# Cosformer attention feeding a leaky-relu feed-forward: 96 partitions of 6 tokens, one-pass leaky relu, and a hand-written order of all engines, on one Trainium2 core

## The chip, the cores and the metric

The kernel runs on one core of a Trainium2 chip. The metric is the device time of one execution in microseconds, measured outside the profiler; the profile's span of the same execution is about 2 us shorter. Ratios are the mean time of one kernel's fast runs over the mean time of the other's fast runs of the same rounds, so they are not quite the ratio of the medians that are quoted.

Names: PE is TensorE's matmul side and PEld its weight loads, DVE is VectorE, ACT is ScalarE, POOL is GpSimd, SP is SyncE. `L204` is line 204 of the kernel in question. Line numbers differ between kernels. In the attention, `kp` and `qp` are phi(k) and phi(q), made by the k and q prep passes; `vex` is v in 16 bit, made by `vcast`; `den`, `rden` and `xs` are the denominator, its reciprocal and the quotient.

## The reference, cut to what matters

```python
# q, k, v: (8 batches, 8 heads, 576 tokens, 64); w_in: (512, 2048); w_out: (2048, 512), all float32
theta = np.pi / 2 * np.arange(S) / S
def phi(x):                                   # 64 -> 128 features
    r = np.maximum(x, 0.0)
    return np.concatenate([r * cos(theta), r * sin(theta)], axis=-1)
kv  = einsum('bhsf,bhsd->bhfd', phi(k), v)    # per head 128 x 64
z   = phi(k).sum(axis=2)
num = einsum('bhsf,bhfd->bhsd', phi(q), kv)
den = einsum('bhsf,bhf->bhs', phi(q), z)[..., None] + 1e-6
x   = (num / den).transpose(0, 2, 1, 3).reshape(4608, 512)
h   = x @ w_in
out = np.maximum(0.01 * h, h) @ w_out
```

The feed-forward is the large part: 9 groups of 512 tokens, each with 64 matmuls for the first layer and 64 for the second. A batch of 576 tokens is a little longer than a group, so attention of batch g+1 must be finished before the first layer of group g+1 begins.

## The kernel before

Attention splits 576 tokens into two chunks of 128 partitions x 2 tokens and one of 64 x 1. For each piece `q` is transposed on PE (`ps_qt`), copied to SBUF (`qpT`), multiplied with `kv` (`pnum`), divided on VectorE (`xs`), transposed back (`ps_xt`) and copied into `xT`. The feed-forward needs two passes for the leaky relu, has three PSUM banks for the first layer (`psh`) and one for the second (`pso`). A scheduler orders the instructions of all engines.

```python
psh_pool = ctx.enter_context(tc.tile_pool(name="ps_h", bufs=3, space=PSUM))
pso_pool = ctx.enter_context(tc.tile_pool(name="ps_o", bufs=1, space=PSUM))
# ... cut ...
def emit_b1(t):                               # first layer of group t
    for m in range(NFT):                      # 16 tiles of 4 matmuls
        psh = psh_pool.tile([P, GRP], dt.float32, name="psh")
        # ... 4 matmuls into psh ...
        hsb = hpool.tile([P, GRP], dt.float32, name="hsb")
        nc.scalar.copy(hsb, psh)
        g = gpool.tile([P, GRP], dt.float16, name="g")
        nc.vector.scalar_tensor_tensor(
            out=g, in0=psh, scalar=0.01, in1=hsb, op0=ALU.mult, op1=ALU.max)
def emit_b2(t, gs):                           # second layer
    for tt in range(4):
        pso = pso_pool.tile([P, DM], dt.float32, name="pso")
        # ... 16 matmuls into pso ...
        osb = opool.tile([P, DM], dt.float32, name="osb")
        nc.vector.tensor_copy(osb, pso)       # then stored to DRAM
# ... cut ...
for bb in range(B + 1):                       # the main loop
    # ... issue loads: k, v of batch bb+1, q of batch bb; with bb == 0 all weights as well ...
    if bb >= 1: phase2(bb - 1, q_stage[bb - 1])      # q side of attention
    if bb < B:  phase1(bb, *kv_stage[bb])            # k, v side
    while groups_done < NGRP and (groups_done + 1) * GRP <= bb * S:
        gs_ = emit_b1(groups_done); emit_b2(groups_done, gs_); groups_done += 1
```

Of the kernel before, what the change touches and what calls it, by code (L numbers as in the profile page):

```python
# [9 lines left out]
dt = mybir.dt  # L11
# [3 lines left out]
P = 128  # L15
# [3 lines left out]
def kernel(  # L19
# [15 lines left out]
    assert F == P and DM == 4 * P and DFF % P == 0 and NT % 512 == 0  # L35
    assert S == 576

    chunk3 = [(0, P, 2), (2 * P, P, 2), (4 * P, S - 4 * P, 1)]
    JMAX = 2
    subs = []  # L40
    for c_, (s0_, npc_, Jc_) in enumerate(chunk3):
        for j_ in range(Jc_):
            subs.append((c_, j_, npc_))
    NSUB = len(subs)
    NC3 = len(chunk3)

    def slot_base(c, j):
        s0, npc, Jc = chunk3[c]
        return s0 + j * npc
# [5 lines left out]
    NE = D + 2  # L55

    const = ctx.enter_context(tc.tile_pool(name="const", bufs=1))
    ident32 = const.tile([P, P], dt.float32, name="ident32")
    make_identity(nc, ident32)
    ident16 = const.tile([P, P], dt.float16, name="ident16")  # L60
    nc.vector.tensor_copy(ident16, ident32)

    w_ang = math.pi / 2.0 / S
    bias_pi2 = const.tile([P, 1], dt.float32, name="bias_pi2")
# [3 lines left out]
    iotaA = const.tile([P, 2, 2], dt.float32, name="iotaA")  # L68
    nc.gpsimd.iota(
        iotaA,  # L70
        pattern=[[2 * P, 2], [1, 2]],
        base=0,
        channel_multiplier=2,
        allow_small_or_imprecise_dtypes=True,
    )
    iotaB = const.tile([P, 1], dt.float32, name="iotaB")
    nc.gpsimd.iota(
        iotaB,
        pattern=[[1, 1]],
        base=4 * P,  # L80
        channel_multiplier=1,
        allow_small_or_imprecise_dtypes=True,
    )
    cosA = const.tile([P, 2, 2], dt.float32, name="cosA")
    sinA = const.tile([P, 2, 2], dt.float32, name="sinA")
    nc.scalar.activation(cosA, iotaA, AF.Sin, bias=bias_pi2, scale=w_ang)
    nc.scalar.activation(sinA, iotaA, AF.Sin, bias=bias_zero, scale=w_ang)
    ntail = chunk3[2][1]
    cosB = const.tile([P, 1], dt.float32, name="cosB")
    sinB = const.tile([P, 1], dt.float32, name="sinB")  # L90
    nc.scalar.activation(
        cosB[0:ntail], iotaB[0:ntail], AF.Sin, bias=bias_pi2[0:ntail], scale=w_ang
    )
    nc.scalar.activation(
        sinB[0:ntail], iotaB[0:ntail], AF.Sin, bias=bias_zero[0:ntail], scale=w_ang
    )

    def cos_col(c, j, npc):
        return cosA[0:npc, c, j : j + 1] if c < 2 else cosB[0:npc, 0:1]

    def sin_col(c, j, npc):
        return sinA[0:npc, c, j : j + 1] if c < 2 else sinB[0:npc, 0:1]

    xT = const.tile([P, NKC, NT], dt.float16, name="xT")
    onesJ = const.tile([P, H, JMAX, 2], dt.float32, name="onesJ")
    nc.vector.memset(onesJ, 1.0)

    w1 = const.tile([P, NKC, DFF], dt.float16, name="w1")
    w2 = const.tile([P, NFT, DM], dt.float16, name="w2")

    def load_w1_slice(c):
        nc.gpsimd.dma_start(w1[:, c, :], moe_w_in[c * P : (c + 1) * P, :])

    def load_w2_slices(ms):
        for m in ms:
            nc.gpsimd.dma_start(w2[:, m, :], moe_w_out[m * P : (m + 1) * P, :])

    kstage = ctx.enter_context(tc.tile_pool(name="kstage", bufs=NC3 + 1))
    vstage = ctx.enter_context(tc.tile_pool(name="vstage", bufs=NC3 + 1))
    qstage = ctx.enter_context(tc.tile_pool(name="qstage", bufs=NC3 + 2))  # L120
    vexpool = ctx.enter_context(tc.tile_pool(name="vext", bufs=1))
    kppool = ctx.enter_context(tc.tile_pool(name="kpp", bufs=NC3 + 2))
    qppool = ctx.enter_context(tc.tile_pool(name="qpp", bufs=NC3))
    qptpool = ctx.enter_context(tc.tile_pool(name="qpT", bufs=4))
    kvpool = ctx.enter_context(tc.tile_pool(name="kvsb", bufs=2))
    xpool = ctx.enter_context(tc.tile_pool(name="xs", bufs=4))
    small = ctx.enter_context(tc.tile_pool(name="small", bufs=3))
    hpool = ctx.enter_context(tc.tile_pool(name="hsb", bufs=2))
    gpool = ctx.enter_context(tc.tile_pool(name="gpool", bufs=NFT + 3))
    opool = ctx.enter_context(tc.tile_pool(name="osb", bufs=2))  # L130
    pskx = ctx.enter_context(tc.tile_pool(name="ps_kvx", bufs=1, space=bass.MemoryType.PSUM))
    psqt = ctx.enter_context(tc.tile_pool(name="ps_qt", bufs=1, space=bass.MemoryType.PSUM))
    psnum = ctx.enter_context(tc.tile_pool(name="ps_num", bufs=1, space=bass.MemoryType.PSUM))
    psh_pool = ctx.enter_context(tc.tile_pool(name="ps_h", bufs=3, space=bass.MemoryType.PSUM))
    pso_pool = ctx.enter_context(tc.tile_pool(name="ps_o", bufs=1, space=bass.MemoryType.PSUM))

    vex_sets = []
    for parity in range(2):
        sset = []
        for c, (s0, npc, Jc) in enumerate(chunk3):  # L140
            vx = vexpool.tile(
                [P, H, Jc, NE], dt.float16, name=f"vex_{parity}_{c}", uniquify=False
            )
            nc.vector.tensor_copy(vx[0:npc, :, :, D:NE], onesJ[0:npc, :, 0:Jc, :])
            sset.append(vx)
        vex_sets.append(sset)

    kv_tiles = {}
    kv_stage = {}
    q_stage = {}  # L150

    def issue_kv_loads(b):
        ksts = []
        vsts = []
        for c, (s0, npc, Jc) in enumerate(chunk3):
            kst = kstage.tile([P, H, Jc, D], dt.float32, name="kst")
            nc.sync.dma_start(  # L157
                kst[0:npc],
                k[b, :, s0 : s0 + Jc * npc, :].rearrange(
                    "h (p j) d -> p h j d", j=Jc  # L160
                ),
            )
            vst = vstage.tile([P, H, Jc, D], dt.float32, name="vst")
            nc.sync.dma_start(  # L164
                vst[0:npc],
                v[b, :, s0 : s0 + Jc * npc, :].rearrange(
                    "h (p j) d -> p h j d", j=Jc
                ),
            )
            ksts.append(kst)  # L170
            vsts.append(vst)
        return ksts, vsts

    def issue_q_loads(b):
        qsts = []
        for c, (s0, npc, Jc) in enumerate(chunk3):
            qst = qstage.tile([P, H, Jc, D], dt.float32, name="qst")
            nc.sync.dma_start(
                qst[0:npc],
                q[b, :, s0 : s0 + Jc * npc, :].rearrange(  # L180
                    "h (p j) d -> p h j d", j=Jc
                ),
            )
            qsts.append(qst)
        return qsts

    def phase1(b, ksts, vsts):
        kps = []
        vexs = []
        for c, (s0, npc, Jc) in enumerate(chunk3):  # L190
            kp = kppool.tile([P, H, Jc, F], dt.float16, name="kp")
            for j in range(Jc):
                nc.scalar.activation(  # L193
                    kp[0:npc, :, j, 0:D],
                    ksts[c][0:npc, :, j, :],
                    AF.Relu,
                    bias=bias_zero[0:npc],
                    scale=cos_col(c, j, npc),
                )
                nc.vector.tensor_scalar(  # L200
                    out=kp[0:npc, :, j, D:F],
                    in0=ksts[c][0:npc, :, j, :],
                    scalar1=0.0,
                    scalar2=sin_col(c, j, npc),  # L204
                    op0=ALU.max,
                    op1=ALU.mult,
                )
            kps.append(kp)
            vex = vex_sets[b % 2][c]
            nc.vector.tensor_copy(vex[0:npc, :, :, 0:D], vsts[c][0:npc])  # L210
            vexs.append(vex)
        kv_sb = kvpool.tile([P, H, NE], dt.float16, name="kv_sb")
        for hg in range(2):
            ps_kv = pskx.tile([P, 4, NE], dt.float32, name="ps_kv", tag="pskx")
            for hh in range(4):
                h = hg * 4 + hh
                for i, (c, j, npc) in enumerate(subs):
                    nc.tensor.matmul(  # L218
                        ps_kv[:, hh, :],
                        lhsT=kps[c][0:npc, h, j, :],  # L220
                        rhs=vexs[c][0:npc, h, j, :],
                        start=(i == 0),
                        stop=(i == NSUB - 1),
                    )
            nc.scalar.copy(kv_sb[:, hg * 4 : hg * 4 + 4, :], ps_kv)
        kv_tiles[b] = kv_sb
# [208 lines left out]
```

## Time and profile before

| | |
|---|---|
| median time, first measurement (3 runs) | 388.69 us |
| first attention matmul / first feed-forward matmul | 30.73 us / 55.79 us |
| 64 second-layer matmuls of a group at full pace | 4 x 3.45 us = 13.8 us |
| last matmul to end of span | 4.5 us |
| mean granted TensorE clock | 0.989 |

The first lines are from the profile page: busy time of the engines, then the chain of work that ended last (followed back from the last instruction to what released each step), by engine and by line.

```profile
...
PE 329.0 (85%) x2272; PEld 172.6 (44%) x2272; DVE 218.2 (56%) x454; ACT 173.8 (45%) x285; POOL 11.7 (3%) x28
...
PE 79%; DVE 6%; SPq 6%; DMA 4%; ACT 3%; issue 1%; ACTq 0%
PE psh L343 34%; PE pso L363 33%; PE ps_kv L218 5%; DVE osb L371 4%; SPq L164 3%; PE ps_qt L257 3%; DMA kst<-in_k_dram 3%; PE ps_xt L296 3%; SPq L157 2%; ACT qpT L263 2%; PE pnum L270 2%; DMA qst<-in_q_dram 1%; DVE xs L284 1%; ACT xT L302 1
...
```

PE holds 79% of the chain. Its two feed-forward lines are 67% of the span; no other engine comes near. The VectorE copy `osb` (L371) stands in the chain with 4%, which means that PE work was released by it. Next, groups of instructions from the same page: engine, operation, shapes, count, then busy time and mean ns of one, then idle time of the engine before them.

```profile
...
L353 DVE SCALAR_TENSOR_TENSOR g<-psh,hsb 128x512 f16<-128x512 f32 x144 | 97.9, 688 | 33.2 <-ACT hsb L351 32.1
L351 ACT COPY hsb<-psh 128x512 f32<-128x512 f32 x144 | 83.2, 585 | 50.8 <-PE psh L343 48.9
...
L371 DVE COPY osb<-pso 128x512 f32<-128x512 f32 x36 | 24.9, 692 | 87.7 <-PE pso L363 87.7
L263 ACT COPY qpT<-ps_qt 128x1024 f16<-128x1024 f16 (+1 forms) x40 | 37.1, 929 | 54.9 <-PE ps_qt L257 53.8
...
```

The leaky relu costs 585 ns on ACT and then 688 ns on DVE per tile; a tile's four matmuls take 0.864 us on PE. Last, what PE itself waited for (total us, times, longest), and a stretch of the timeline (start, duration, engine and line, count, wait before).

```profile
...
PE ps_kv L218 <- DVE kp L200: 31.3, 4, 30.7
PE ps_qt L257 <- ACT qpT L263: 10.3, 11, 1.2
PE pso L363 <- DVE osb L371: 4.7, 9, 0.8
...
```

```profile
...
122.84 0.42 PE L270 MATMUL pnum<-kv_sb,qpT 128*128 128x66 f16 x8
123.19 0.41 PE L257 MATMUL ps_qt<-ident_63,qp 64*128 64x64 f16 x8
123.78 3.61 PE L363 MATMUL pso<-w_85,g 128*128 128x512 f16 x16 [0.19 <-DVE osb L371]
127.23 0.39 PE L296 MATMUL ps_xt<-ident_63,xs 128*128 128x128 f16 x4
127.45 0.42 PE L270 MATMUL pnum<-kv_sb,qpT 128*128 128x66 f16 x8
...
```

When the 16 matmuls of one `pso` tile are done, PE does a few attention matmuls (`pnum`, `ps_qt`, `ps_xt`) while VectorE copies the tile, and so it hardly waits: 4.7 us in nine waits. The VectorE copy `osb` is on the chain with about 16.7 us.

### The profile page before, as it was taken

Reading aid. Unit: us, or ns where it says so; the run is one execution under the profiler, and the core shown is the slowest. Engines: PE = TensorE matmul, PEld = TensorE weight load, DVE = VectorE, ACT = ScalarE, POOL = GpSimd, SP = SyncE. Lnnn points to the kernel's source line nnn. Section 1 sums busy time; section 2 is a strip of 40 time slices with the busy share of each in tenths; the row PEclk is TensorE's granted clock in tenths of the full one; section 3 lists DMA queues with packets and bytes.
Section 4 is the critical chain, followed back from the end, with each engine's and each line's share of the span. In section 5 each row is a group of like instructions: output and inputs, shape, how many; then the busy total and the mean of one; then the engine's idle time right before and its main releaser. Section 6 shows DMA issues by size and latency. Waiting matters only on the chain.

```text
span 388.8 us, 5799 instructions
## 1 busy us (share of the span) xinstructions
PE 329.0 (85%) x2272; PEld 172.6 (44%) x2272; DVE 218.2 (56%) x454; ACT 173.8 (45%) x285; POOL 11.7 (3%) x28
## 2 busy tenths in 40 slices
PE   0004479997899999989999999899999999999984
PEld 0003455455444554455455545554455455444431
DVE  0006858945696369555955783566467427733711
ACT  3014556624583248326832672455256426612600
POOL 6230000000000000000000000000000000000000
PEclk9999999999899999998999999999999999999999
DMA  8999998567572418232604302100120031011022
GB/s 203 214 212 306 338 311 193 158 187 207 149 206 64 110 29 235 74 112 69 189 29 110 81 0 56 67 2 1 56 54 2 3 73 36 0 54 56 1 55 54
DMA packets 71003, 42.31 MB, mean 109 GB/s; under 512 B 14656, under 2 KB 65856, under 8 KB 70976
## 3 DMA queue, kind: packets, MB, share of 16 engines
q1 hardware_dynamic: 68096, 37.76, 35.4%
q0 software_dynamic: 2880, 4.20, 5.9%
q8 instruction: 17, 0.28, 0.3%
q14 instruction: 10, 0.08, 0.1%
HBM read 36.70 MB, written 9.44 MB: 119 GB/s over the span
## 4 chain that ended last, share of the span: by engine, by line
PE 79%; DVE 6%; SPq 6%; DMA 4%; ACT 3%; issue 1%; ACTq 0%
PE psh L343 34%; PE pso L363 33%; PE ps_kv L218 5%; DVE osb L371 4%; SPq L164 3%; PE ps_qt L257 3%; DMA kst<-in_k_dram 3%; PE ps_xt L296 3%; SPq L157 2%; ACT qpT L263 2%; PE pnum L270 2%; DMA qst<-in_q_dram 1%; DVE xs L284 1%; ACT xT L302 1%; ACT kp L193 0%
## 5 line engine op out<-in xcount | busy, mean ns | idle before, releaser
L343 PE MATMUL psh<-xT,w_84 128*128 128x512 f16 x576 | 139.0, 387 | 0.2
L363 PE MATMUL pso<-w_85,g 128*128 128x512 f16 x576 | 133.2, 379 | 5.9 <-DVE osb L371 4.7
L353 DVE SCALAR_TENSOR_TENSOR g<-psh,hsb 128x512 f16<-128x512 f32 x144 | 97.9, 688 | 33.2 <-ACT hsb L351 32.1
L351 ACT COPY hsb<-psh 128x512 f32<-128x512 f32 x144 | 83.2, 585 | 50.8 <-PE psh L343 48.9
L363 PEld LDWEIGHTS <-g 128*128 128x128 f16 x576 | 56.2, 98 | 71.7 <-issue 8.4
L343 PEld LDWEIGHTS <-w_84 128*128 128x128 f16 x576 | 54.0, 99 | 61.7 <-issue 3.6
L371 DVE COPY osb<-pso 128x512 f32<-128x512 f32 x36 | 24.9, 692 | 87.7 <-PE pso L363 87.7
L263 ACT COPY qpT<-ps_qt 128x1024 f16<-128x1024 f16 (+1 forms) x40 | 37.1, 929 | 54.9 <-PE ps_qt L257 53.8
L218 PE MATMUL ps_kv<-vex_0,kp 128*128 128x66 f16 x128 | 15.5, 204 | 31.8 <-DVE kp L200 30.9
L302 ACT COPY xT<-ps_xt 128x512 f16<-128x512 f16 (+1 forms) x40 | 21.8, 545 | 44.4 <-PE ps_xt L296 43.7
L257 PE MATMUL ps_qt<-ident_63,qp 128*128 128x128 f16 (+1 forms) x320 | 26.3, 225 | 14.6 <-ACT qpT L263 10.3
L218 PEld LDWEIGHTS <-kp 128*128 128x128 f16 (+1 forms) x320 | 19.3, 99 | 42.7 <-issue 33.8
L193 ACT ACTIVATE kp<-kst,bias_zero,cosA 128x512 f16<-128x512 f32 x32 | 25.7, 818 | 19.2 <-DMA kst<-in_k_dram 19.2
L257 PEld LDWEIGHTS <-qp 128*128 128x128 f16 (+1 forms) x320 | 20.8, 103 | 19.2 <-issue 11.7
L284 DVE TENSOR_TENSOR xs<-pnum,rden 128x512 f16<-128x512 f32 (+1 forms) x40 | 27.4, 686 | 0.8
L270 PE MATMUL pnum<-kv_sb,qpT 128*128 128x66 f16 (+1 forms) x320 | 19.1, 202 | 0.0
L296 PE MATMUL ps_xt<-ident_63,xs 128*128 128x128 f16 (+1 forms) x160 | 16.1, 228 | 2.0 <-DVE xs L284 2.0
L296 PEld LDWEIGHTS <-xs 128*128 128x128 f16 (+1 forms) x160 | 11.1, 103 | 13.2 <-DVE xs L284 6.5
L270 PEld LDWEIGHTS <-qpT 128*128 128x128 f16 (+1 forms) x320 | 15.7, 107 | 2.7 <-issue 0.4
L235 DVE TENSOR_SCALAR qp<-qst,cosA 128x512 f16<-128x512 f32 x32 | 15.2, 474 | 1.6 <-PE ps_qt L257 0.8
L218 PE MATMUL ps_kv<-vex_1,kp 128*128 128x66 f16 x128 | 15.0, 199 | 0.4 <-DVE kp L200 0.4
L200 DVE TENSOR_SCALAR kp<-kst,sinA 128x512 f16<-128x512 f32 x32 | 14.3, 476 | 1.6 <-DMA kst<-in_k_dram 1.6
(34 smaller groups left out, 96.1 us busy)
## 6 DMA issues: line engine op xcount, KB each, us to landing
kst<-in_k_dram SPq DMA_DIRECT2D x16, 512.0 KB, 5.0
vst<-in_v_dram SPq DMA_DIRECT2D x16, 512.0 KB, 6.0
qst<-in_q_dram SPq DMA_DIRECT2D x16, 512.0 KB, 4.6
out_dram<-osb SPq DMA_DIRECT2D x40, 128.0 KB, 2.4
out_dram<-osb SPq DMA_DIRECT2D x16, 256.0 KB, 2.5
w_84<-in_moe_w_in_dram POOLq DMA_DIRECT2D x4, 512.0 KB, 10.3
w_85<-in_moe_w_out_dram POOLq DMA_DIRECT2D x16, 128.0 KB, 7.3
kst<-in_k_dram SPq DMA_DIRECT2D x8, 128.0 KB, 4.6
```

Of the source, the lines that this page charges most:

```text
L193: nc.scalar.activation(kp[0:npc, :, j, 0:D], ksts[c][0:npc, :, j, :], AF.Relu, bias=bias_zero[0:npc], scale=cos_col(c, j, npc),)
L218: nc.tensor.matmul(ps_kv[:, hh, :], lhsT=kps[c][0:npc, h, j, :], rhs=vexs[c][0:npc, h, j, :], start=(i == 0), stop=(i == NSUB - 1),)
L257: nc.tensor.transpose(ps_qt[:, h, 0:npc], qp[0:npc, h, j, :], ident16[0:npc, 0:npc],)
L263: nc.scalar.copy(qpT[:, :, 0:npc], ps_qt[:, :, 0:npc])
L270: nc.tensor.matmul(pnum[0:npc, h // 4, (h % 4) * NE : (h % 4) * NE + NE], lhsT=qpT[:, h, 0:npc], rhs=kv_sb[:, h, :],)
L284: nc.vector.tensor_tensor(out=xs[0:npc].rearrange("p (a b) e -> p a b e", a=2), in0=pnum[0:npc, :, 0 : 4 * NE].rearrange("p a (b e) -> p a ...
L296: nc.tensor.transpose(ps_xt[:, jj, 0:npc], xs[0:npc, 2 * jj : 2 * jj + 2, :], ident16[0:npc, 0:npc],)
L343: nc.tensor.matmul(psh, lhsT=w1[:, c, m * P : (m + 1) * P], rhs=xT[:, c, t * GRP : (t + 1) * GRP], start=(c == 0), stop=(c == NKC - 1),)
L351: nc.scalar.copy(hsb, psh)
L353: nc.vector.scalar_tensor_tensor(out=g, in0=psh, scalar=0.01, in1=hsb, op0=ALU.mult, op1=ALU.max)
L363: nc.tensor.matmul(pso, lhsT=gs[m][:, tt * P : (tt + 1) * P], rhs=w2[:, m, :], start=(m == 0), stop=(m == NFT - 1),)
L371: nc.vector.tensor_copy(osb, pso)
```

## The change

Its intent is to keep PE busy with feed-forward matmuls all the time and to slip the attention of batch g+1 between those of group g, in a fixed pattern of 32 slots of four matmuls. For that it makes the token layout uniform (6 tokens on each of 96 partitions), does the leaky relu in one ScalarE pass, gives `pso` a second bank (and `psh` two instead of three), moves PSUM copies between engines, fixes the order of every engine's queue, and arranges the loads so that batch 0 comes first, then weights, then batch 1. The core of the diff, with cuts marked:

```diff
-    chunk3 = [(0, P, 2), (2 * P, P, 2), (4 * P, S - 4 * P, 1)]
+    J = 6; NP = S // J                        # 6 tokens on 96 partitions
-    psh_pool ... bufs=3      pso_pool ... bufs=1
+    psh_pool ... bufs=2      pso_pool ... bufs=2
+    ctx.enter_context(tc.manual_schedule())
+    def load(name, b, half, after=None):      # 96 partitions, runs of 3 tokens = 768 bytes
+        if after is not None:                 # a one-element copy makes the load wait
+            nc.gpsimd.tensor_copy(t[0:1, 0, 0, 0:1], after)
+        nc.sync.dma_start(t, view[:, :, half * JH : (half + 1) * JH, :])
 ... cut: set-up; loads of batch 0, then w1 and w2 in four pieces each, gated on v of batch 0 ...
     # leaky relu
-    nc.scalar.copy(hsb, psh)
-    nc.vector.scalar_tensor_tensor(out=g, in0=psh, scalar=0.01, in1=hsb, op0=ALU.mult, op1=ALU.max)
+    nc.scalar.activation(gt, psh, AF.Prelu, bias=bias_zero, scale=1.0, alpha=0.01)
-    nc.vector.tensor_copy(osb, pso)           # output copy
+    nc.scalar.copy(osb, pso)
-    nc.scalar.copy(qpT, ps_qt)                # likewise xT
+    nc.vector.tensor_copy(t, ps)
 ... cut: attention of batch 0 ...
+    def period(g):                            # group g, attention of batch b = g + 1
+        if b < B:
+            slots[0].append(lambda: kv_mm(b, 0)); slots[1].append(lambda: kv_mm(b, 1))
+            for j in range(J):
+                slots[4 * j].append(lambda j=j: prep("q", b, j, "dve"))
+                slots[4 * j + 2].append(lambda j=j: t_step(b, j))      # q transposes
+                slots[4 * j + 4].append(lambda j=j: n_step(b, j))      # numerator, then den, rden, xs
+                slots[4 * j + 7].append(lambda j=j: x_step(b, j))      # transposes back
+        if b + 1 < B:                         # loads, vcast and k prep of the batch after
 ... cut ...
+        for s in range(32):
+            ffn1(g, s) if s < 16 else ffn2(g, (s - 16) // 4, s % 4)    # 4 matmuls
+            for f in slots[s]: f()
+    for name in ("k", "v", "q"):
+        for half in range(2):
+            load(name, 1, half, after=w2[0:1, NFT // 2 - 1, 0:1])      # after half of w2
+    # k prep and vcast of batch 1 here, then
+    for g in range(NGRP): period(g)
```

## The prediction

> **What bounds the kernel now.** TensorE: in the chain of waits that ended last (span 388.8 us) it holds 79%, feed-forward matmuls 34% + 33%. In the timeline 16 of those issue in 3.45 us, 0.216 us each, so all 1152 need 249 us. The rest:
> - Start: no matmul until 30.7 us, no feed-forward until 55.8 us. DMA is 80 to 99% busy there; weights, k, v and q share it.
> - Output copy: one pso buffer, so most tiles wait for the VectorE copy (0.70 us); 4.3% of the chain, 16.7 us.
> - Attention: qpT copies (1.01 us) make PE wait 10.3 us.
> - Last matmul to end: 4.5 us.
>
> **What the change does.**
> 1. Leaky relu: copy (585 ns) + VectorE pass (688 ns) become one ScalarE pass.[...] It frees VectorE (98 us).[...]
> 2. Two pso buffers, copy on ScalarE: the 16.7 us go.
> 3. 96 x 6 instead of 128/128/64: 48 kv, 48 + 24 transposes, 48 numerator matmuls per batch, against 40/40/20/40. The break at 64-row kv matmuls ([...]full-row ones start about 33 ns apart) goes. Estimate per batch: kv 1.7, q transposes 2.1, numerator 2.8 (64-column weights were 46 ns apart; I take 59 for 96), x transposes 1.0: 7.6 us, about as before.
> 4. Attention of batch g+1 inside the matmuls of group g. Each period has 27.65 us of feed-forward, periods 0 to 6 add 7.6. New wait: after a numerator step VectorE does den, rden, xs (1.15 us) and two q preps (0.9 us), while PE has two slots (1.73 us) before the next q transpose: about 0.35 us, five of six steps. With vcast 2.2 us per period. Period: 37.5 us; periods 7 and 8: 28.5 each.
> 5. VectorE copies qpT[...]. The trace has no such copy; f32 took 692 ns.
> 6. Start: batch 0's k, v, q first (3.5 MB at the 330 to 346 GB/s seen), then weights[...], batch 1's loads only after half of w2. Batch 1's k prep precedes the first Prelu, and its kv matmuls stand in slots 0 and 1, so period 0 waits for its k and v: weights half way at 31 us, v at 46. PE starts at the slow early pace (8 transposes took 1.04 us at first, 0.61 later): effectively 48 us, 8 before the old start.
>
> **Sum.** 48 + 7 x 37.5 + 2 x 28.5 + 4.5 = 372; wait 4 may be shorter: 368 us, range 355 to 380. Faster by over 2% 0.88, within 2% 0.10, slower 0.02.
>
> **What would show it.** Timeline: second psh tile at 44 to 50 us, after ps_kv waited for batch 1's v; PE waits: ps_qt on DVE qp about 30 times, 0.35 us each; pso on its copy gone; Prelu 650 to 720 ns; periods (windows) 35 to 38.5 and 28 to 29 us.
>
> **What would make it wrong.** DMA at the start off by 5 us; VectorE falling behind[...], so that periods pass 39 us; numerator matmuls at 33 ns; granted clock below 0.989.

The marked cuts are terms that no trace or run of this case shows: the estimate for the Prelu and the wait per slot that followed from it, the estimates for the `qpT` copy on VectorE, a time for five kv matmuls, and the rate that I had counted on for the weights. The sum came to 372 us, of which I announced 368: 48 for the start, 7 x 37.5 and 2 x 28.5 for the periods, 4.5 for the tail. 28.5 is 27.65 of feed-forward plus 0.85 for the waits per slot, and the 31 and 46 us behind the 48 used the rate for the weights.

## The result, and the profile after

| | before | after |
|---|---|---|
| median time, same rounds (4 runs each) | 389.59 us | 371.29 us |
| ratio, 95% interval | | 0.9549 (0.9509 to 0.959): faster |
| span of the profiled run | 388.8 us | 369.6 us |
| mean granted clock | 0.989 | 0.998 |

The page of the changed kernel, the same lines as before:

```profile
...
PE 320.6 (87%) x2496; PEld 170.6 (46%) x2496; DVE 165.8 (45%) x393; ACT 169.2 (46%) x259; POOL 8.8 (2%) x22
...
PE 64%; DVE 19%; DMA 11%; issue 2%; POOL 1%; SPq 1%; ACT 0%; POOLq 0%; ACTq 0%; DVEq 0%
PE pso L257 26%; PE psh L230 24%; DMA vst<-in_v_dram 7%; PE ps_qt L181 6%; DVE xs L204 5%; DMA w_141<-in_moe_w_out_dram 4%; DVE qp L146 4%; DVE qp L150 4%; PE pnum L192 3%; PE ps_kv L169 3%; DVE rden L202 2%; PE ps_xt L215 2%; DVE vex L157
...
L238 ACT ACTIVATE g<-psh,bias_zero 128x512 f16<-128x512 f32 x144 | 98.9, 687 | 61.4 <-PE psh L230 61.4
...
L184 DVE COPY qpT<-ps_qt 128x768 f16<-128x768 f16 x48 | 26.7, 556 | 59.7 <-PE ps_qt L181 59.7
...
```

PE is still what bounds the kernel, but VectorE has come into the chain with 19%, all of it attention work (`xs`, `qp`, `rden`, `den`). The one-pass relu takes 687 ns, the `qpT` copy on VectorE 556 ns for 768 16-bit elements. No DVE copy is left in front of `pso`.

What PE waited for:

```profile
...
PE ps_kv L169 <- DVE vex L157: 29.4, 4, 12.9
PE ps_qt L181 <- DVE qp L150: 9.6, 35, 0.3
...
```

The wait of `pso` is gone. There is a new one, `ps_qt` on the VectorE `qp` pass, 35 times (the start wait, `ps_kv`, is nearly as long as before). One of these 35 in the timeline, from the numerator matmuls to the next q transposes:

```profile
...
64.43 0.51 PE L192 MATMUL pnum<-kv_sb,qpT 128*96 128x66 f16 x8
...
64.78 1.89 PE L230 MATMUL psh<-xT,w_140 128*128 128x512 f16 x8
64.98 0.16 DVE L198 TENSOR_SCALAR den<-pnum 96x8 f32<-96x8 f32 x1 [0.85 <-PE pnum L192]
...
65.41 0.69 DVE L204 TENSOR_TENSOR xs<-pnum,rden 96x512 f16<-96x512 f32 x1
...
66.02 0.47 DVE L146 TENSOR_SCALAR qp<-qst,cos_t 96x512 f16<-96x512 f32 x1
66.41 0.48 DVE L150 TENSOR_SCALAR qp<-qst,sin_t 96x512 f16<-96x512 f32 x1
...
66.94 0.52 PE L181 MATMUL ps_qt<-ident,qp 96*128 96x96 f16 x8 [0.27 <-DVE qp L150]
...
```

PE has eight feed-forward matmuls to do (64.78 to 64.78 + 1.73 = 66.51 us, at 0.216 us each), while VectorE works through den, rden, xs and both q passes in the order in which they were written. PE starts the transposes at 66.94 us: 0.43 us late. (The view calls only 0.27 us idle, because it models how long a matmul's end takes; start-to-start distances are the safer reading.)

The start, in the chain in order of time (start, duration, what):

```profile
...
2.32 11.14 DMA vst<-in_v_dram
...
18.62 15.71 DMA w_141<-in_moe_w_out_dram
36.30 14.39 DMA vst<-in_v_dram
50.79 0.97 DVE vex L157
...
```

Batch 0's v lands at 13.46 us, the gate of batch 1's loads (second quarter of w2) opens at 34.33 us, batch 1's v lands at 50.69 us, and only then does the kernel come into its pattern. Last, busy time of each engine in two whole periods, one with attention and one without (from:to, length, PE, PEld, DVE, ACT, POOL, clock, DMA share, GB/s):

```profile
...
126.70:163.18 36.48, 35.11 (x297) 18.82 (x296) 20.41 (x50) 18.33 (x28) 0.00 (x0) 1.00 0.59 127
337.23:365.38 28.15, 28.13 (x129) 12.23 (x126) 0.00 (x0) 13.33 (x20) 0.00 (x0) 1.00 0.16 38
...
```

The sum can now be taken from the trace. Group 0's period ends, and group 1's begins, at 90.21 us; six periods take 36.48 us each to 309.11 us; the last two, without attention, 28.1 us each, to 365.38 us; the tail is 4.2 us. Counting back one period of 36.48 from 90.21 puts the effective start at 53.7 us, against 55.8 in the kernel before. From there to the last matmul it takes 311.6 us, against 328.5 before (55.79 to 384.26). So about 17 of the 19 us in the span come from the steady part, 2 from the start.

### The profile page after: what moved, and what is told of

It reads as the page before. It is cut to its first block, busy times and chain, and to the rows that moved or that the text cites. A ratio compares the mean times of both kernels' runs of the same rounds, so it can differ in the third digit from the quotient of the medians.

```text
span 369.6 us, 6024 instructions
## 1 busy us (share of the span) xinstructions
PE 320.6 (87%) x2496; PEld 170.6 (46%) x2496; DVE 165.8 (45%) x393; ACT 169.2 (46%) x259; POOL 8.8 (2%) x22
## 4 chain that ended last, share of the span: by engine, by line
PE 64%; DVE 19%; DMA 11%; issue 2%; POOL 1%; SPq 1%; ACT 0%; POOLq 0%; ACTq 0%; DVEq 0%
PE pso L257 26%; PE psh L230 24%; DMA vst<-in_v_dram 7%; PE ps_qt L181 6%; DVE xs L204 5%; DMA w_141<-in_moe_w_out_dram 4%; DVE qp L146 4%; DVE qp L150 4%; PE pnum L192 3%; PE ps_kv L169 3%; DVE rden L202 2%; PE ps_xt L215 2%; DVE vex L157 2%; DVE den L198 2%; POOL w_140 L126 1%
## 5 line engine op out<-in xcount | busy, mean ns | idle before, releaser
L238 ACT ACTIVATE g<-psh,bias_zero 128x512 f16<-128x512 f32 x144 | 98.9, 687 | 61.4 <-PE psh L230 61.4
L266 ACT COPY osb<-pso 128x512 f32<-128x512 f32 x36 | 21.1, 585 | 100.4 <-issue 52.4
L184 DVE COPY qpT<-ps_qt 128x768 f16<-128x768 f16 x48 | 26.7, 556 | 59.7 <-PE ps_qt L181 59.7
L142 ACT ACTIVATE kp<-kst,bias_zero,cos_t 96x512 f16<-96x512 f32 x48 | 36.8, 807 | 12.3 <-DMA kst<-in_k_dram 12.3
L181 PE MATMUL ps_qt<-ident,qp 96*128 96x96 f16 x384 | 26.5, 216 | 11.4 <-DVE qp L150 9.6
L204 DVE TENSOR_TENSOR xs<-pnum,rden 96x512 f16<-96x512 f32 x48 | 32.9, 686 | 1.6
L169 PEld LDWEIGHTS <-kp 96*128 96x128 f16 x384 | 16.0, 106 | 34.3 <-ACT g L238 13.8
L192 PEld LDWEIGHTS <-qpT 128*96 128x96 f16 x384 | 26.0, 133 | 11.9 <-DVE xs L204 3.1
L192 PE MATMUL pnum<-kv_sb,qpT 128*96 128x66 f16 x384 | 26.4, 216 | 2.0 <-DVE xs L204 2.0
L150 DVE TENSOR_SCALAR kp<-kst,sin_t 96x512 f16<-96x512 f32 x48 | 22.0, 472 | 10.8 <-DMA kst<-in_k_dram 10.8
L150 DVE TENSOR_SCALAR qp<-qst,sin_t 96x512 f16<-96x512 f32 x48 | 23.4, 488 | 1.5 <-DMA qst<-in_q_dram 1.5
## 6 DMA issues: line engine op xcount, KB each, us to landing
w_141<-in_moe_w_out_dram POOLq DMA_DIRECT2D x4, 512.0 KB, 16.7
```

The lines of the kernel that those rows point to most:

```text
L142: nc.scalar.activation(t[:, :, 0:D], src, AF.Relu, bias=bias_zero[0:NP], scale=cos_t[:, j : j + 1])
L150: nc.vector.tensor_scalar(out=t[:, :, D:F], in0=src, scalar1=0.0, scalar2=sin_t[:, j : j + 1], op0=ALU.max, op1=ALU.mult,)
L169: nc.tensor.matmul(ps[:, hh, :], lhsT=kps[b, j][:, h, :], rhs=vex[b % 2][:, j, h, :], start=(j == 0), stop=(j == J - 1),)
L181: nc.tensor.transpose(ps[:, h, :], qps[b, j][:, h, :], ident[0:NP, 0:NP])
L184: nc.vector.tensor_copy(t, ps)
L192: nc.tensor.matmul(pn[0:NP, h // HH, (h % HH) * NE : (h % HH) * NE + NE], lhsT=qpTs[b, j][:, h, :], rhs=kvs[b][:, h, :],)
```

## The experiments

Twelve kernels ran, all with correct results. Times are medians of four runs, except for the probe. The changed kernel was not run again beside them: differences to its 371.29 us compare different rounds, in which the kernel before had medians of 388.5 to 389.6 us.

### 1. `e1_qprep_early`: the q passes two slots earlier

```diff
-    slots[4 * j].append(lambda j=j: prep("q", b, j, "dve"))
+    slots[max(0, 4 * j - 2)].append(lambda j=j: prep("q", b, j, "dve"))
```

> One edit: the two q preps of step j are issued on VectorE two slots earlier (slot 4j-2 instead of 4j), so the q transposes find qp ready. Theory (the order of VectorE's own queue makes PE wait): the gap of 0.43 us before five q transposes per period goes, 2.2 us per period, periods 34.3 us instead of 36.5, total about 356 us. Rival (VectorE or PE has no room, the wait comes back at the numerator step or at vcast): periods stay at 36 us or more, total 368 to 372.

Measured: 355.79 us, ratio 0.9147 (0.9111 to 0.9183) to the kernel before. The same stretch in windows:

```profile
...
121.85:156.11 34.26, 34.26 (x297) 19.24 (x296) 19.96 (x50) 18.34 (x28) 0.00 (x0) 1.00 0.61 135
...
```

A period is 34.26 us instead of 36.48, and `ps_qt` no longer waits for `qp` at all. Seven times 2.2 us is 15.5 us, and the median fell by 15.5 us. The theory holds, and so the wait was a matter of order alone: VectorE does the same work, 19.96 us of busy time in a period against 20.41.

### 2. `e8_scheduler`: without the fixed order

```diff
-    ctx.enter_context(tc.manual_schedule())
```

> The changed kernel with the manual_schedule line taken out, so that the scheduler may reorder the engines. The built program shows that it keeps the interleaving of the source on PE nearly everywhere. Theory (the order that matters is the program's, the flag adds little): 368 to 375. Rival (fixing all engine queues by hand is itself worth the gain): 385 or more.

Measured: 359.80 us, ratio 0.9258 (0.9213 to 0.9302). Both expectations missed: it is 11.5 us faster than with the order fixed by hand. The instruction order of the built program shows the scheduler putting VectorE's q passes ahead of the den, rden, xs of the step before or between them, and the trace has no wait of `ps_qt` on `qp` left; the ends of groups with attention lie 34.3 to 35.7 us apart, against 36.48. So the scheduler found most of the repair of `e1_qprep_early` by itself. Freezing this order by hand was not useful; what the interleaving of the source is worth, apart from layout and loads, no run shows.

### 3. `e9_order_only`: layout and order, without what they were given

Relu in two passes, `psh` 3 banks, `pso` 1, as in the kernel before; the layout and the order as in the changed one.

```diff
-    psh bufs=2, pso bufs=2
+    psh bufs=3, pso bufs=1
-    nc.scalar.activation(gt, psh, AF.Prelu, bias=bias_zero, scale=1.0, alpha=0.01)
+    nc.scalar.copy(hsb, psh)
+    nc.vector.scalar_tensor_tensor(out=gt, in0=psh, scalar=0.01, in1=hsb, op0=ALU.mult, op1=ALU.max)
```

> Layout and hand order of the changed kernel, but relu in two passes and the banks of before (psh 3, pso 1): the order without what it was given. Theory (the hand order puts 5.5 us of VectorE work against 4.7 us of PE work per step in stage 1, and keeps the output copy wait): 395 to 410, slower than before. Rival (the order is the gain, relu and banks are side matters): 375 to 385.

Measured: 412.84 us, ratio 1.0635 (1.0599 to 1.0671). Layout and order without those two are slower than the kernel before by 24 us. PE's two large waits in the pattern:

```profile
...
PE ps_qt L182 <- DVE qp L151: 33.8, 35, 1.2
...
PE pso L262 <- ACT osb L271: 14.6, 27, 0.7
...
```

With the relu pass in VectorE's queue an attention step of the first layer takes 5.64 us (one q transpose at 151.16 us, the next at 156.80) against 4.76 us in the changed kernel, and the three `pso` tile changes inside each group wait for the copy.

### 4. `e2_two_pass_relu`: the changed kernel with the two-pass relu

```diff
-    nc.scalar.activation(gt, psh, AF.Prelu, bias=bias_zero, scale=1.0, alpha=0.01)
+    nc.scalar.copy(hsb, psh)
+    nc.vector.scalar_tensor_tensor(out=gt, in0=psh, scalar=0.01, in1=hsb, op0=ALU.mult, op1=ALU.max)
```

> The leaky relu of before (ScalarE copy, then VectorE pass) put back into the changed kernel, all else kept. Theory (the one pass matters because a psh buffer comes free sooner): copy 0.585 + pass 0.688[...] hold a buffer 1.7 us after its matmuls, against 0.9 us with one pass; with two buffers a slot then takes about 1.28 us instead of 0.864 where no attention stands between: +40 to +60 us, 410 to 430. Rival (as my prediction had it, the one pass only frees VectorE, which is 45% busy): under 380.

(The marked cut is a time for the two hand-overs, which the traces do not show as told. My estimates of 1.7 and 1.28 us contain it.)

Measured: 411.45 us, ratio 1.0569 (1.0508 to 1.0631), inside the theory's range, but only in part for its reason. What PE waited for:

```profile
...
PE ps_qt L182 <- DVE qp L151: 26.4, 35, 1.2
PE psh L231 <- DVE g L241: 10.1, 28, 0.5
...
```

The timeline in a period without attention:

```profile
...
340.83 1.89 PE L231 MATMUL psh<-xT,w 128*128 128x512 f16 x8
...
342.51 0.69 DVE L241 SCALAR_TENSOR_TENSOR g<-psh,hsb 128x512 f16<-128x512 f32 x1 [4.58 <-ACT hsb L240]
342.76 0.59 ACT L240 COPY hsb<-psh 128x512 f32<-128x512 f32 x1 [0.28 <-PE psh L231]
343.26 1.89 PE L231 MATMUL psh<-xT,w 128*128 128x512 f16 x8 [0.54 <-DVE g L241]
...
345.68 1.89 PE L231 MATMUL psh<-xT,w 128*128 128x512 f16 x8 [0.53 <-DVE g L241]
...
```

PE starts a pair of tiles every 2.42 us (343.26, 345.68), 1.21 us per tile, where it needs 0.864. The first buffer of a pair is free only when the second pass has read it, which ends at 342.51 + 0.69 = 343.20 us, and PE starts at 343.26. Its four matmuls take from 340.83 to 341.69 us (4 x 0.216), so the buffer is held 1.51 us after them, not 1.7. In the changed kernel 64 first-layer matmuls without attention take 14.31 us, 0.894 us per tile. This is the theory's wait (`psh` on `g` in the view), but the two periods without attention bring only 8.7 of the 40 us (32.5 us each against 28.1).

The rest arises in the periods with attention: 41.15 us against 36.48. There PE waits above all for `qp`, 26.4 us in 35 pieces against 9.6, because the relu passes stand in VectorE's queue. `e9_order_only` separates the two causes, since it has the two-pass relu with a third `psh` bank. From its first matmul to that of the second layer, the first layer with attention takes 22.15 us there (136.03 to 158.18), 23.22 us here (135.98 to 159.20) and 19.53 us in the changed kernel (126.53 to 146.06); the second layer takes 17.92 us here and 16.95 in the changed kernel. So of 4.67 us per period about 1.1 belong to the bank and 3.6 to VectorE's queue. My estimate by this subtraction, over all periods: about 25 of the 40 us for VectorE, about 15 for the bank. The pass on ScalarE is worth 40 us in this kernel for both reasons, and VectorE's relief, which my prediction had named, is the larger one in this hand-written order. No run had the two-pass relu together with the early q passes of experiment 1.

### 5. `e3_one_pso`: one bank for the second layer

```diff
-    pso_pool = ctx.enter_context(tc.tile_pool(name="ps_o", bufs=2, space=PS))
+    pso_pool = ctx.enter_context(tc.tile_pool(name="ps_o", bufs=1, space=PS))
```

> pso pool with one buffer instead of two. Theory (the output copy waits that before showed are worth what its chain said, 16.7 us): PE waits about 0.65 us at three of four tile changes per group, 27 in all, plus nothing at the fourth: +15 to +18 us, total 386 to 389. Rival (attention steps between the tiles hide the copy): under 376.

Measured: 390.77 us, ratio 1.0047 (1.0004 to 1.0091): 19.5 us more than the changed kernel.

```profile
...
PE pso L257 <- ACT osb L266: 15.6, 27, 0.7
...
```

27 waits, as expected, of 0.6 us each by the view; start to start a tile change without attention costs 0.88 us (338.63, 342.96, 347.29 us are successive tile starts, 3.45 us of work each), which is why the total is a little above the expectation. The second bank is worth as much as the whole gain over the kernel before.

### 6. `e6_before_prelu` and `e7_before_relu_pso2`: the same two parts in the kernel before

The first is the kernel before with the one-pass relu alone. The second also moves the bank.

```diff
-    nc.scalar.copy(hsb, psh)
-    nc.vector.scalar_tensor_tensor(out=g, in0=psh, scalar=0.01, in1=hsb, op0=ALU.mult, op1=ALU.max)
+    nc.scalar.activation(g, psh, AF.Prelu, bias=bias_zero, scale=1.0, alpha=0.01)
     # e7_before_relu_pso2 also:
-    psh bufs=3, pso bufs=1
+    psh bufs=2, pso bufs=2
```

> The kernel before with only the leaky relu in one ScalarE pass, and the PSUM bank that this makes spare moved from psh (3 to 2) to pso (1 to 2); order and layout as before, the scheduler's. Theory (the output copy wait is worth its 4.3% of the chain): 371 to 376 us. Rival (what the change won came from the order by hand): 385 to 390.

> The kernel before with only the leaky relu in one ScalarE pass; banks (psh 3, pso 1), order and layout as before. This splits e7_before_relu_pso2, which was 19 us slower than before although its output copy waits were gone. Theory (moving the bank let the scheduler run the 64 second-layer matmuls in one piece, and leave the attention steps that had filled the copy waits to stand alone): relu alone stays at 384 to 392. Rival (the relu pass itself changed the scheduler's order for the worse): 400 or more.

Measured: relu alone 387.89 us, ratio 0.9975 (0.9935 to 1.0016), the same. Relu and bank 407.45 us, ratio 1.0465 (1.0394 to 1.0536): slower, which neither of my expectations for that run had. Its waits and its timeline:

```profile
...
PE ps_qt L257 <- ACT qpT L263: 20.6, 25, 1.3
...
```

```profile
...
243.51 12.25 PE L359 MATMUL pso<-w,g 128*128 128x512 f16 x56
255.59 0.61 PE L257 MATMUL ps_qt<-ident,qp 128*128 128x128 f16 x8
257.36 0.61 PE L257 MATMUL ps_qt<-ident,qp 128*128 128x128 f16 x8 [1.16 <-ACT qpT L263]
...
```

The wait of `pso` is gone, but 56 second-layer matmuls now run in one piece, and the attention steps that had filled the pauses between tiles stand alone behind them: from 255.59 to 263.13 us PE does nothing but attention steps and waits between them, up to 1.16 us at a time, and the waits for `qpT` are 20.6 us in 25 pieces, against 10.3 us in 11 before. In `e6_before_prelu` the attention steps still stand between the tiles, at 269.97 us and 274.37 us for instance, between `pso` runs of 16:

```profile
...
274.37 0.61 PE L257 MATMUL ps_qt<-ident,qp 128*128 128x128 f16 x8
...
275.31 3.61 PE L359 MATMUL pso<-w,g 128*128 128x512 f16 x16
...
```

The pair shows that the move of the bank, not the relu, changed the scheduler's order. (It also took the third `psh` bank away; the two were not tried apart. The granted clock, 0.969 to 0.983 against 0.996 to 0.999 in `e6_before_prelu`, was lower too, which by my estimate from these clocks could explain some 2% of the 5%.) A wait that is filled with other work is not time to be won.

### 7. `e10_dma_probe`, `e5_runs512` and `e4_gate_w1`: the loads of the start

I had counted with 330 to 346 GB/s for batch 0's loads. The windows of the changed kernel show 235 GB/s from 5 to 10 us, with nothing but k, v and q on the engines. Two things had changed: runs of 768 bytes instead of 512, and 96 partitions instead of 128.

```diff
 # e5_runs512: three parts of two tokens, 512-byte runs, on the same 96 partitions
-    JH = J // 2
+    JH = 2
 # e10_dma_probe: in front of everything, the k pattern (768-byte runs, 1536 bytes between partitions)
+    for i in range(2): nc.sync.dma_start(scr[:, i], rows_i[:, :, 0:JH, :])         # 128 partitions
+    # ... when that has landed:
+    for i in range(2): nc.sync.dma_start(scr2[:, i], rows_i[0:96, :, 0:JH, :])     # 96 of the same
 # e4_gate_w1: batch 1's loads wait for w1 instead of half of w2
-    after=w2[0:1, NFT // 2 - 1, 0:1]
+    after=w1[0:1, 0, DFF - 1 : DFF]
```

(The probe has fewer `g` and `osb` buffers, to make room.)

> k, v, q staged in three parts of two tokens instead of two of three, so that the runs in DRAM are 512 bytes on the same 96 partitions. Theory A (768-byte packets are what made the loads slow: 56 ns against 27 ns for the 512-byte packets of before): loads reach about 340 GB/s, batch 0's v lands near 9.5 us instead of 13.5, first kv matmuls of batch 1 near 43 instead of 52 us, total about 362. Theory B (96 partitions are what made them slow): loads stay at 230 GB/s, total 370 to 373.

> The changed kernel with two stages of loads put in front, alone on the DMA engines: first two loads of the same pattern as its k loads (768-byte runs, 1536 bytes from partition to partition) on 128 partitions, 1.57 MB, then the same on 96 partitions, 1.18 MB. Theory (the partition count sets the rate): 330 to 345 GB/s and about 36 ns per packet in the first stage, 220 to 240 GB/s and 56 ns in the second. Rival (the run length or the stride in DRAM sets it): 220 to 240 GB/s in both. The total time is of no interest.

> Batch 1's loads are gated on the last quarter of w1 instead of the second quarter of w2. Theory (the DMA engines are busy all the time from 2 to 60 us, so the order of the bytes matters little): v of batch 1 lands at 48 to 50 us instead of 50.8, total 369 to 371. Rival (the gate holds the loads back while engines have room): v lands near 44, total about 364.

Measured: `e5_runs512` 372.78 us, ratio 0.9595 (0.9527 to 0.9662), no gain. By its window from 5 to 10 us (223 GB/s at a DMA share of 1.18 over 16 engines) its 512-byte packets took about 43 ns each, against 27 ns for those of the kernel before (median in the trace; 56 ns for the 768-byte ones of the changed kernel, 5 to 13 us). V of batch 1 landed no earlier: its last cast starts at 51.3 us, 50.8 in the changed kernel. The probe, one run of 386.45 us that is of no interest as a time, in windows of 2 us inside its two stages:

```profile
...
4.00:6.00 2.00, 0.00 (x0) 0.00 (x0) 0.00 (x0) 0.00 (x0) 0.00 (x0) 1.00 1.09 348
12.00:14.00 2.00, 0.00 (x0) 0.00 (x0) 0.00 (x0) 0.00 (x0) 0.00 (x0) 1.00 1.10 232
...
```

On 128 partitions the loads move 348 GB/s, on 96 partitions of the same rows 232 GB/s, two thirds; by these rates and shares a packet took about 38 and 58 ns. So the partition count sets the rate here. No run varied which partitions are used, so the mechanism stays open.

`e4_gate_w1`: 371.04 us, ratio 0.9529 (0.9485 to 0.9572), no change beyond noise. The last cast of batch 1's v starts at 49.7 us instead of 50.8. In the changed kernel the DMA share is above 1.1 in every window of 5 us from 5 to 60 us, so the engines are never short of work, and opening one gate earlier only exchanges one load for another.

### 8. `e11_start` and `e12_start_w2`: a start that needs less

Since bytes are what the start lacks, the remedy is to need fewer of them before the feed-forward begins: load batch 0, w1, batch 1, w2 in this order, and move all attention steps some slots later, so that the first tiles of group 0 need only batch 0 and w1. Both also have the early q passes of experiment 1.

```diff
+    for name in ("k", "v", "q"):              # between w1 and w2
+        for half in range(2): load(name, 1, half, after=w1[0:1, 0, DFF - 1 : DFF])
+    nc.gpsimd.tensor_copy(w2[0:1, 0, 0:1], staged["q", 1, 1][0:1, 0, 0, 0:1])   # e12: staged["v", 1, 1]
     # ... w2's loads ...
+    OFF = 7                                   # e12: 8
+    # slots counted through all groups: attention of batch b starts at slot 32 * (b - 1) + OFF;
+    # batch 1's k prep on VectorE in slots 0 to 5; k and v of batch 2 gated on the end of w2
```

> Start rebuilt, q preps early: loads in the order batch 0, w1, batch 1, w2; batch 1's k prep moved to VectorE in slots 0 to 5 of the first period; every attention step 7 slots later, so that the first seven feed-forward tiles need nothing of batch 1. Theory (17 us of the 51 us before the feed-forward were spent on waiting for batch 1's k and v): second psh tile at 35 to 36 us instead of 53, a wait of 2 to 5 us for w2 at slots 16 to 19, periods 34.3 us, total 338 to 346. Rival (DMA cannot deliver w2 in time, the wait only moves): 350 or more.

> As e11_start, but w2 is requested once batch 1's v has landed instead of its q, and attention is 8 slots later instead of 7. In e11 q landed at 48.6 us and w2 only from 55 to 63 us, while feed-forward at full clock wants it from about 52 us. Theory (that wait is where e11 lost 6 to 9 us of what I expected): w2 all landed by 60 us, a wait of 4 to 6 us left, total 344 to 348. Rival (the loads share the engines, so q comes later by what w2 comes earlier): 349 to 352 as e11.

`e11_start`: fast runs of 349.8 to 352.5 us, ratio 0.9017 (0.8946 to 0.9088): two of the three lie in the rival's range (350 or more), one just under it. One of its four executions, the profiled one, took 480.05 us at a mean granted clock of 0.683. What caused that is not recorded. It is left out of the ratio, and of its trace I use only when w2 was requested: from 49.1 us on, after q had landed. No rerun of that kernel gave a fast trace, so where its missing 6 to 9 us went was an inference when I wrote the next expectation.

`e12_start_w2` tested it: 347.59 us (four fast runs, 346.57 to 347.82), ratio 0.8942 (0.8915 to 0.897), inside the expected range. It is the best version, 10.6% under the kernel before. What PE still waits for w2 in it, and its start in the timeline:

```profile
...
PE pso L261 <- DMA w<-in_moe_w_out_dram: 2.1, 2, 1.2
...
```

```profile
...
34.84 10.07 PE L234 MATMUL psh<-xT,w 128*128 128x512 f16 x36 [0.57 <-ACT xT L226]
44.74 0.89 PE L173 MATMUL ps_kv<-vex,kp 96*128 96x66 f16 x24
...
56.64 1.02 PE L261 MATMUL pso<-w,g 128*128 128x512 f16 x4 [0.96 <-DMA w<-in_moe_w_out_dram]
...
59.16 1.82 PE L261 MATMUL pso<-w,g 128*128 128x512 f16 x4 [1.16 <-DMA w<-in_moe_w_out_dram]
...
```

The first 36 feed-forward matmuls run from 34.84 us, before any attention of batch 1. They take 10.07 us, where 36 x 0.216 would be 7.8. In the changed kernel, too, the first tile's four matmuls took 1.86 us (at 34.39 us), where four took 1.02 at 56.64 us above. The clock views do not settle it: 1.00 from 34.39 to 36.25 us in the changed kernel, whose trace has no clock record before 57.6 us, and the digit 9 in this stretch of the page of `e12_start_w2`. That page's one digit 8 is the slice from 60.5 to 69.2 us, and around it four matmuls took 1.82 us (at 59.16 us, after the second wait) and 1.79 us (at 61.11 us). The cause is not shown, and no run tested it. Two waits for w2 are left.

## Why the prediction was right or wrong

The predicted time was 368 us, range 355 to 380, "faster" at 0.88; the result is 371.29 us. The total was right in part by luck: two terms of the sum were wrong by 5.7 and 7 us and cancelled. The sum itself was 372; the 4 us taken off because the VectorE wait "may be shorter" did not come. Point by point:

1. **Start: the term that failed.** "Batch 0's k, v, q first (3.5 MB at the 330 to 346 GB/s seen)" and "weights half way at 31 us, v at 46 ... effectively 48 us". Measured: 34.3, 50.7 and 53.7 us. The order of events was as told (gate, v, cast, `ps_kv`), but the rate came from loads on 128 partitions; on 96 it is 232 to 235 GB/s. The probe shows it (348 against 232 GB/s). The announced gain of 8 us at the start was 2, and the second `psh` tile began at 52.92 us, not at 44 to 50.
2. **Numerator matmuls: mis-sized in the other direction.** I took 59 ns each for 96-column weights. In the timeline above eight of them fill 64.43 to 64.78 us, 44 ns each. For 128-column weights it was 33 ns in the kernel before (127.45 to 127.71 us). The spacing does not simply follow the columns: the 46 ns for 64 columns, from which I went up to an estimate of 59, include the step to the next kind of matmul (eight in 138.48 to 138.85 us), and among themselves those stand 33 ns apart. Why 96 columns take longer than either, no run shows. The kv matmuls took 30 ns (24 in 127.39 to 128.12 us), so 1.45 us per batch instead of 1.7; in the kernel before, a group of five with one of 64 rows took 0.36 us (62.01 to 62.37 us). In all, attention takes 6.6 us of a period, not 7.6.
3. **The VectorE wait: right.** "About 0.35 us, five of six steps", 2.2 us per period with vcast; measured 0.43 us, 35 times, 2.2 us per period. The sum agrees partly by luck: each wait was longer than told, and vcast added none (it ran at 146.54 us, and the wait before the transposes at 149.43 us is 0.43 us like the others). `e1_qprep_early` shows that it is this order and nothing else. Period 36.48 us against 37.5 predicted; the difference is point 2.
4. **Prelu: right in size, incomplete in what it is worth.** 687 ns (mean of 144), inside the recorded range of 650 to 720. "It frees VectorE (98 us)" is the larger part of what it is worth in the changed kernel, about 25 of 40 us by the estimate in experiment 4; the other part, which I had not named, is that two banks do for `psh`. In the kernel before, with three banks, it is worth nothing (`e6_before_prelu`).
5. **"Two pso buffers ... the 16.7 us go": right in the changed kernel only.** Taking the bank away costs 19.5 us there. In the kernel before, moving it over from `psh` makes the kernel slower by 20 us (407.45 against 387.89), because those waits were hiding attention. As a reading of the profile before, the step was wrong: time on the chain that another step fills is not free time.
6. **VectorE's qpT copy: measured.** 556 ns for 768 16-bit elements from PSUM (mean of 48), less than the 692 ns for 512 of 32 bit in the kernel before. The sum had no term for this copy.
7. **Clock and tail: as assumed.** The clock was 0.998, the tail 4.2 us.

What came of the parts, then: the layout and order alone cost 24 us, relu and bank alone cost 19 us, and together they gain 18. Layout and order were never tried apart from each other. None of the parts explains the gain by itself.

## What to carry to other kernels

Before counting a wait as time to be won, look in the timeline at what runs inside it, and try parts of a change together as well as alone: here each half was slower than nothing. When an engine's order is fixed by hand, write each producer as early as its buffers allow, not next to its consumer; two slots were worth 15 us. Measure a load's rate in the shape that the new layout will have, since a rate read from another partition count was off by a third (348 GB/s on 128 partitions, 232 on 96).
